# Down products by output block and attention on four PSUM banks in an attention + two-FFN kernel

## The chip, the cores and the metric

The kernel runs on one core of a Trainium2 chip. The metric is the device time of one execution in microseconds (us); lower is better. A profile is one further execution, recorded instruction by instruction. Engines are named as in the profile: PE (TensorE matmul), PEld (its weight loads), DVE (VectorE), ACT (ScalarE), POOL (GpSimd) and SP (the queue that issues nearly all DMAs).

## The reference

Attention over 4 batches of 8 heads (576 positions, 64 wide), whose output, 2304 tokens of 512 features, goes through two gated feed-forward networks in a row; the first normalises its input by RMS. Everything is float32.

```python
def _attn_ref(q, k, v):
    scores = scale * np.matmul(q, k.transpose(0, 1, 3, 2))
    mask_local = (rel >= 0) & (rel < 32)
    mask_strided = (rel >= 0) & (pos[None, :] % 32 == pos[:, None] % 32)
    masks = np.stack([mask_local if h < H // 2 else mask_strided for h in range(H)], axis=0)
    scores = np.where(masks[None], scores, -1000000000.0)
    attn = softmax(scores)
    return np.matmul(attn, v)

def _moe_ref(x, w_gate, w_val, w_out, rms_g):
    xn = x / rms * rms_g
    g = xn @ w_gate
    silu = g * (1.0 / (1.0 + np.exp(-g)))
    return silu * (xn @ w_val) @ w_out
```

The second network is the same without the normalisation. The hidden width is 1536, that is 12 chunks of 128.

## The kernel before, in words

**Products.** Each float32 product is made of three products of a high and a low part (`hi`, `lo`), so a 128x128 block of weights against n tokens is three matmuls. A *chunk* is 128 hidden features: its *gate* products (bank `g`, or `a0` late) and *value* products (bank `v`, or `a1`) are 12 matmuls each, and its *down* products are 3 matmuls for each of the four output blocks j (128 output features, banks `y0` to `y3`).

**Stages.** (1) Attention of batch 0 alone. (2) Attention of batches 1 to 3 woven into chunks 0 to 3 of the first network, which run over six token *segments* (`early`, L39: 256, 256, 512, 512, 256, 512 tokens). (3) What is left: passes over chunks 4 to 11 of the first network and 0 to 11 of the second, in steps of 768 tokens. The first of them (called pass 0 below) follows the last segment at once. Only stage 2 and its border with pass 0 are touched.

**What sets the order in stage 2.** `gate` (L976) and `down` (L998) call `point()` (L176) after every few matmuls. A point is a *place*: there one phase of each running attention step is issued (`advance`, L97), new steps are started as `pace["att"]` allows (0.9 a place in segments 0 and 1, 1.3 from segment 2 on, L1186), one small operation of the x sums in `due` may be issued, and one operation of a weight step of `late` (paced by `pace["op"]`). Every engine then executes its own instructions in the order in which they stand.

**Attention steps.** Scores (S, `kT,qT`), softmax on DVE (L664), ACT (L673), DVE (L683, L684) and POOL (L690), transposes of the softmax `e` (T, L69), their copy to `pT` on ACT (L76), products with v (V, `pT,vl` or `pT,vs`) and their copy to `x`. The transposes of q and k are copied to `qT` and `kT` by ACT and DVE. Each S, T or V takes a bank from `att.tags` in turn (`abank`, L498). In stage 1 these are all eight banks, in stage 2 the two banks `a0` and `a1` (L1080).

**Down products.** `run` (L1090) issues the down products of a chunk two chunks later, all four j on banks `y0` to `y3`, which collect over the four chunks of a segment. After the fourth, `finish` (L1014) copies the four banks to `ob` buffers (DVE for even j, ACT for odd j) and sends them to DRAM; until attention is over, `ob` shares three buffers (tag `s`) with the gate's own temporary `sg`.

**Weights.** `room[4]` is the list of 4 KB places for split weights, 13 at first, 5 more when attention's memory is freed and 2 more before pass 0. `plan` (L1069) lists the weight steps: `d` splits a down weight, `p` splits the seven combined gate and value weights of a chunk and parks them in DRAM (`pk`), `r` recalls them. `ahead_x` (L1112) makes sums of x early, from a pool `px` with two buffers for each of four tags.

Of the kernel before, what the change touches and what calls it, by code (L numbers as in the profile page):

```python
# [8 lines left out]
F32 = mybir.dt.float32  # L9
F32R = mybir.dt.float32r  # L10
# [15 lines left out]
def attn_ffn_ffn(ctx: ExitStack, tc: tile.TileContext, q, k, v, w1g, w1v, w1o, rms_g, w2g, w2v, w2o, out):  # L26
# [38 lines left out]
    def product(out_, a, b_, start, stop, **how):  # L65
        traced(nc.tensor.matmul(out_, a, b_, start=start, stop=stop, **how))  # L66
# [4 lines left out]
    def bank(tag):  # L71
        return pp.tile([128, 512], F32, tag=tag, name=f"b_{tag}")
# [103 lines left out]
    def point():  # L176
        advance()
        if state["early"]:
            some_x()
        weights()  # L180
        for nm, src in (("dec", wq), ("att", steps)):
            if state["hold"] and nm == "dec":
                continue
            have[nm] = min(have[nm] + pace[nm], 2.0)
            while have[nm] >= 1.0 and src and src[0].ready():
                have[nm] -= 1.0
                start(src.pop(0))
# [12 lines left out]
    wt = {}  # L200
    wdone = set()

    room = {4: [(wpa, f"u{i}") for i in range(13)], 2: []}
    held = {}
    order = [(m, c) for m in (1, 2) for c in range(FC)]

# [257 lines left out]
    def need_w(m, c, z):  # L464
        drain(wq, lambda: (m, c, z) in wdone or not wq and not any(st.prio == PRIO_W for st in active))
        while (m, c, z) not in wdone:
            if begun:
                operate(begun[0])
            else:
                prefetch(True)  # L470
# [505 lines left out]
    def gate(m, c, n, xs, final=False):  # L976
        need_w(m, c, 0)
        gv = GV[0]
        GV.append(GV.pop(0))
        pg = bank(gv[0])  # L980
        proj(pg, n, wt[m, c, 0], xs)
        hp, w = pools["h"]
        s = hp.tile([128, w], F32, tag="s", name="sg", bufs=3)
        silu(s, pg, n)
        point()
        need_w(m, c, 1)
        pv = bank(gv[1])
        proj(pv, n, wt[m, c, 1], xs)
        if final:
            hh, hl = (pools["ob"][0].tile([128, 512], F32R, tag="ob", name=nm) for nm in ("hh", "hl"))  # L990
        else:
            hh = hp.tile([128, w], F32R, tag="hh", name="hh", bufs=3)
            hl = hp.tile([128, w], F32R, tag="hl", name="hl", bufs=3)
        hidden(s, pv, hh, hl, n)
        point()
        return hh, hl
# [59 lines left out]
    def plan(text):  # L1056
        for word in text.split():
            m, c = int(word[1]), int(word[2:])
            kind = word[0]
            if kind in "dq":  # L1060
                late.append(weight_step(m, c, 2, kind == "q"))
            elif kind == "s":
                late.append(recall_out(m, c))
            elif kind == "r":
                late.append(recall_step(m, c))
            else:
                late.append(combined_step(m, c, {"c": "keep", "h": "split", "p": "park"}[kind]))

    plan("d14 p14 p15 p16 p17 r14 d15 r15 d16 r16 d17 r17 c18 d18 p19 p110 p111 r19 d19 r110 d110 r111 d111 "  # L1069
         "c20 d20 p21 p22 p23 r21 d21 r22 d22 r23 d23 c24 d24 p25 p26 p27 r25 d25 r26 d26 r27 d27 c28 d28 p29 p210 p211 r29 d29 r210 d210 r211 d211")  # L1070
    att.consts()
    for b in range(B):
# [2 lines left out]
    for i in range(1000):  # L1075
# [1 line left out]
            break  # L1077
        pace["dec"] = 0.7 if i >= 0 else 0.0
        point()
    att.tags = ["a0", "a1"]  # L1080
    state["start"] = False
    waiting = []
    with tc.high_priority(offset=PRIO_R):
# [6 lines left out]
    def run(f):  # L1090
        si, c, h = f
        m, t0, n, c0, c1 = segs[si]
        if c == c0:
            ys[:] = [bank(f"y{j}") for j in range(KC)]
        down(m, c, n, ys, h, c == c0, c == c1 - 1)
        if si == last_seg[m, c]:
            used((m, c, True))
        if c == c1 - 1:
            finish(t0, n, ys)

    def there(si):
        if si >= NA or att is None:
            return True
        t0, n = segs[si][1:3]
        return all((b, j) in att.done for b in range(B) for j in range(2) if S * b + parts(b)[j][0] < t0 + n)
# [6 lines left out]
    def ahead_x(t0):  # L1112

        pool = pools["px"][0]
        f = {}
        xsum[1, t0] = {}

        def fetch_(nm, kk):
            def g():
                t = f[nm, kk] = pool.tile([128, HN], F32, tag=nm, name="xst", bufs=2)  # L1120
                k0, o0 = RAW[nm]
                for o, a, w, d in pieces(x_d, t0 + o0, HN):
                    send(out=t[:, o:o + w], in_=d[:, k0 + kk, a:a + w])
            return 0, g

        def add(z, a, b, op, kk):
            def g():
                paced(nc.gpsimd.tensor_tensor(out=f[z, kk], in0=f[a, kk], in1=f[b, kk], op=op))
            return 1, g

        def keep_(i, nm, kk):
            def g():
                d = xsum[1, t0].setdefault(i, [])
                d.append(dp.tile([128, HN], F32, name=f"xq{t0}_{i}_{kk}"))
                send(out=d[kk], in_=f[nm, kk])
            return 0, g

        rest = 1, lambda: None
        todo = [fetch_(nm, kk) for kk in range(2) for nm in ("a21", "a22", "a11", "a12")] + [rest] * 4
        for kk in range(2):  # L1140
            todo += [add("a22", "a21", "a22", ALU.add, kk), keep_(5, "a22", kk), add("a21", "a11", "a21", ALU.subtract, kk), keep_(7, "a21", kk),
                     add("a11", "a22", "a11", ALU.subtract, kk), keep_(6, "a11", kk), add("a12", "a12", "a11", ALU.subtract, kk), keep_(3, "a12", kk)]
        due.extend((0, cost, g) for cost, g in todo)

    def first_x():
# [37 lines left out]
    for si, (m, t0, n, c0, c1) in enumerate(segs):  # L1183
        nxt = segs[si + 1] if si + 1 < len(segs) else None
        loaded = False
        pace["att"] = 0.9 if si < 2 else 1.3  # L1186
        pace["dec"] = 0.25
        pace["op"] = 0.0 if si < 2 else 1.8
        state["late"] = si >= 2
        state["xr"] = 0.8 if si < NA - 1 else 0.4  # L1190
        state["lag"], state["wait"] = (5, 6) if att is None else (2, 3)
        xs = xs_of.pop(si)
        state["tanh"] = True and att is not None
        for c in range(c0, c1):
            for i, t in enumerate((0, 2 * HN)):
                if att is not None and si >= 2 and (1, t) not in xsum and have_x(t + 2 * HN) and (not i or (1, 0) in xsum):
                    ahead_x(t)
                    state["early"] = True
            if nxt_last(si) and c == 0:
                first_x()  # L1200
                state["early"] = True
            h = gate(m, c, n, xs, nxt is None and c == c1 - 1)
            if si == last_seg[m, c]:
                used((m, c, False))
            if len(waiting) >= 2:
                run(waiting.pop(0))
            waiting.append((si, c, h))
            if att and not steps and not active_att():
                if due: print("due left", len(due))
                while due:  # L1210
                    due.pop(0)[2]()
                actx.close()
                close_pools("px")
                att = None
                GV.append(("a0", "a1"))
                open_pool("wpb", "wpb", 0, bufs=1)
                open_pool("ob", "ob", 512, bufs=4)
                room[4] += [(pools["wpb"][0], f"v{i}") for i in range(5)]
                open_pool("x7", "x7", 0, bufs=1)
                room[2] += [(pools["wpb"][0], f"e{i}") for i in range(5)]  # L1220
            if nxt and c >= c1 - 3 and si + 1 not in xs_of:
                if c == c1 - 2 and not there(si + 1):
                    while steps and not there(si + 1):
                        advance()
                        if steps[0].ready() and not there(si + 1):
                            start(steps.pop(0))
                    while not there(si + 1):
                        advance()
                if not loaded and there(si + 1):
                    load_x(*nxt[:3])  # L1230
                    loaded = c
                if loaded is not False and (c > loaded or c == c1 - 1):
                    xs_of[si + 1] = split_x(si + 1)
# [8 lines left out]
    open_pool("xs", "xs", 0, bufs=1, reuse_waits="tile")  # L1242
    open_pool("ob2", "ob2", 512, bufs=3)
    open_pool("wpc", "wpc", 0, bufs=1)
    room[4] += [(pools["wpc"][0], f"w{i}") for i in range(2)]
    x7, xs, tp, obp, obq = (pools[key][0] for key in ("x7", "xs", "t", "ob", "ob2"))
    SETS = (("g", "v", "a0", "a1"), ("y0", "y1", "y2", "y3"))
    passes = [(1, (4, 5, 6, 7)), (1, (8, 9, 10, 11)), (2, (0, 1, 2, 3)), (2, (4, 5, 6, 7)), (2, (8, 9, 10, 11))]
# [387 lines left out]
```

## Time and profile before

| what | value |
|---|---|
| median of 3 runs | 1060.49 us (1058.42 to 1064.2) |
| the profiled execution's own time | 1058.07 us |
| its span, first to last instruction | 1056.3 us |
| PE busy | 986.0 us (93%) |
| PEld busy | 903.9 us (86%) |
| DVE, ACT busy | 582.8 us, 581.8 us (55% each) |
| POOL busy | 394.8 us (37%) |
| mean granted clock of TensorE | 0.970 of full |

The granted clock has two levels here, 2.4 GHz (written 1.00) and 1.2 GHz; a value between them is a stretch that had both. The time lies 1.8 us above the span, and the profiled execution is 2.4 us below the median. A busy PE is read from the row of the slices; where PE waited, and for whom, is read from the waits; a bracket in the timeline, `[2.38 <-ACT pT L76]`, is the idle time before that instruction and what ended it.

### The profile page before, as it was taken

Reading aid. Unit: us, or ns where it says so; the run is one execution under the profiler, and the core shown is the slowest. Engines: PE = TensorE matmul, PEld = TensorE weight load, DVE = VectorE, ACT = ScalarE, POOL = GpSimd, SP = SyncE. Lnnn points to the kernel's source line nnn. Section 1 sums busy time; section 2 is a strip of 40 time slices with the busy share of each in tenths; the row PEclk is TensorE's granted clock in tenths of the full one; section 3 lists DMA queues with packets and bytes.
Section 4 is the critical chain, followed back from the end, with each engine's and each line's share of the span. In section 5 each row is a group of like instructions: output and inputs, shape, how many; then the busy total and the mean of one; then the engine's idle time right before and its main releaser. Section 6 shows DMA issues by size and latency. Waiting matters only on the chain. (4 is left out here: it accounts for less than half of the span.)

```text
span 1056.3 us, 17050 instructions
## 1 busy us (share of the span) xinstructions
PE 986.0 (93%) x5768; PEld 903.9 (86%) x5768; DVE 582.8 (55%) x1297; ACT 581.8 (55%) x1457; POOL 394.8 (37%) x421
## 2 busy tenths in 40 slices
PE   4759988897999999999999999999999999999998
PEld 4548976676798999998999999999998999988997
DVE  3766476565653464546564566654556655563433
ACT  5876675566535464546555456655556555563431
POOL 3212135162105152815253473846335252522400
PEclk9759999989999999999999999999999999999999
DMA  7566265582498647599575959538687567875121
GB/s 193 157 191 193 64 182 190 171 264 85 164 326 285 230 139 251 171 330 308 159 248 171 324 200 320 177 127 297 221 292 225 196 228 278 301 224 180 62 79 60
DMA packets 169967, 218.19 MB, mean 207 GB/s; under 512 B 46996, under 2 KB 123484, under 8 KB 169880
## 3 DMA queue, kind: packets, MB, share of 16 engines
q1 hardware_dynamic: 169688, 216.83, 62.8%
q8 instruction: 45, 0.74, 0.3%
q14 instruction: 42, 0.34, 0.1%
q0 software_dynamic: 192, 0.28, 0.1%
HBM read 145.23 MB, written 71.83 MB: 205 GB/s over the span
## 5 line engine op out<-in xcount | busy, mean ns | idle before, releaser
L1309 POOL TENSOR_TENSOR xl<-xst,xh 128x384 fp32r<-128x384 f32 x196 | 211.4, 1103 | 190.0 <-ACT xh L1308 85.6
L66 PE MATMUL b_y<-xh,w 128*128 128x384 f32 x784 | 211.7, 336 | 4.2 <-DVE t L1376 1.9
L66 PEld LDWEIGHTS b_y<-xh,w 128*128 128x128 f32 x784 | 142.9, 188 | 8.1 <-DVE t L1376 2.3
L66 PE MATMUL b_a<-xh,w 128*128 128x384 f32 (+2 forms) x512 | 141.9, 336 | 2.2 <-ACT t L1366 0.9
L66 PE MATMUL b_y<-xl,w 128*128 128x384 f32 x392 | 131.4, 335 | 0.0
L66 PE MATMUL b_g<-xh,w 128*128 128x384 f32 (+2 forms) x416 | 127.7, 348 | 1.9 <-ACT t L1366 1.2
L66 PE MATMUL b_v<-xh,w 128*128 128x384 f32 (+2 forms) x352 | 110.2, 354 | 0.0
L66 PE MATMUL b_y<-hh,w 128*128 128x384 f32 (+2 forms) x384 | 104.7, 345 | 0.5 <-ACT hh L1390 0.3
L66 PEld LDWEIGHTS b_a<-xh,w 128*128 128x128 f32 x512 | 93.1, 188 | 6.5 <-ACT t L1366 1.8
L1308 ACT CAST xh<-xst 128x384 fp32r<-128x384 f32 x196 | 91.6, 520 | 2.5 <-DMA xst<-x_d 2.5
L66 PE MATMUL b_a<-xl,w 128*128 128x384 f32 (+2 forms) x256 | 85.9, 335 | 0.0
L66 PEld LDWEIGHTS b_g<-xh,w 128*128 128x128 f32 x416 | 77.0, 190 | 7.1 <-ACT t L1366 1.7
L374 POOL TENSOR_TENSOR raw<-dh 128x256 f32<-128x256 f32 x40 | 29.0, 740 | 142.5 <-DVE dh L285 86.5
L66 PEld LDWEIGHTS b_y<-xl,w 128*128 128x128 f32 x392 | 73.6, 188 | 1.7
L66 PEld LDWEIGHTS b_y<-hh,w 128*128 128x128 f32 x384 | 70.0, 191 | 5.9 <-ACT hh L1390 0.6
L690 POOL TENSOR_TENSOR e<-e,rc 128x384 f32<-128x384 f32 (+3 forms) x40 | 38.1, 954 | 94.2 <-DVE rc L684 40.4
L66 PE MATMUL b_g<-xl,w 128*128 128x384 f32 (+2 forms) x208 | 70.5, 339 | 0.0
L66 PEld LDWEIGHTS b_v<-xh,w 128*128 128x128 f32 x352 | 65.5, 191 | 5.2 <-issue 0.4
L66 PE MATMUL b_y<-w,hh 128*128 128x512 f32 x216 | 67.6, 393 | 0.5 <-DVE w L297 0.5
L280 DVE SCALAR_TENSOR_TENSOR raw<-raw 128x512 uint32<-128x512 uint32 x53 | 48.1, 911 | 34.5 <-ACT raw L276 34.4
L66 PE MATMUL b_y<-hl,w 128*128 128x384 f32 (+2 forms) x192 | 65.4, 341 | 0.0
L673 ACT ACTIVATE e<-e,nb 128x96 f32<-128x96 f32 (+2 forms) x152 | 56.4, 375 | 13.9 <-DVE nb L664 13.8
(206 smaller groups left out, 2114.2 us busy)
## 6 DMA issues: line engine op xcount, KB each, us to landing
w<-pk SPq DMA_DIRECT2D x48, 512.0 KB
pk<-raw SPq DMA_DIRECT2D x80, 256.0 KB
raw<-in_moe_w_gate_dram SPq DMA_DIRECT2D x24, 512.0 KB
raw<-in_moe_w_val_dram SPq DMA_DIRECT2D x24, 512.0 KB
raw<-in_moe_w_out_dram SPq DMA_DIRECT2D x24, 512.0 KB
part<-ob SPq DMA_DIRECT2D x48, 256.0 KB
xst<-y_d SPq DMA_DIRECT2D x30, 384.0 KB
xst<-xq SPq DMA_DIRECT2D x28, 384.0 KB
```

What stands on the lines that cost most here:

```text
L66: traced(nc.tensor.matmul(out_, a, b_, start=start, stop=stop, **how))
L280: nc.vector.scalar_tensor_tensor(out=cell["r"], in0=cell["hw"], scalar=0x80000000, in1=cell["r"], op0=ALU.bitwise_and, op1=ALU.bitwise_or)
L374: paced(nc.gpsimd.tensor_tensor(out=t[:, z], in0=a, in1=b, op=ALU.subtract))
L673: r = nc.scalar.activation(out=e[:qn, i, :kn], in_=e[:qn, i, :kn], func=AF.Exp, bias=nb[:qn, i:i + 1], scale=-1.0, accum_out=sums[:qn, i:i ...
L690: eng.tensor_tensor(out=e[:qn, :nt, :kn], in0=e[:qn, :nt, :kn], in1=rc[:qn, :nt].unsqueeze(2).to_broadcast([qn, nt, kn]), op=ALU.mult)
L1308: nc.scalar.copy(out=xh[:, kk], in_=src[:, kk])
L1309: nc.gpsimd.tensor_tensor(out=xl[:, kk], in0=src[:, kk], in1=xh[:, kk].bitcast(F32), op=ALU.subtract)
```

## The change

1. `att.tags` in stage 2 becomes `a0, a1, y2, y3`: four banks for attention.
2. Down products are collected per segment (`kept`) and issued by `by_block` behind the next segment's first gated chunk: for each output block j the 12 matmuls of all four chunks, on `y0` for even j and `y1` for odd j, then that block's copy and store. The last segment keeps the old way. `hh` and `hl` get five buffers instead of three.
3. `pace["att"]` is 1.1 in segments 0 and 1 and 1.7 from segment 2 on.
4. To pay for the buffers, `px` has one buffer per tag (its two halves one after the other, with rests between), and `room[4]` has 12 places at first, 4 more after attention and 4 more before pass 0. Since the thirteenth place is gone, `d14` stands behind `r14` in the plan.

```diff
-    room = {4: [(wpa, f"u{i}") for i in range(13)], 2: []}
+    room = {4: [(wpa, f"u{i}") for i in range(12)], 2: []}
-            hh = hp.tile([128, w], F32R, tag="hh", name="hh", bufs=3)
-            hl = hp.tile([128, w], F32R, tag="hl", name="hl", bufs=3)
+            hh = hp.tile([128, w], F32R, tag="hh", name="hh", bufs=5)
+            hl = hp.tile([128, w], F32R, tag="hl", name="hl", bufs=5)
-    plan("d14 p14 p15 p16 p17 r14 d15 r15 d16 r16 d17 r17 c18 d18 p19 p110 p111 r19 d19 r110 d110 r111 d111 "
+    plan("p14 p15 p16 p17 r14 d14 d15 r15 d16 r16 d17 r17 c18 d18 p19 p110 p111 r19 d19 r110 d110 r111 d111 "
-    att.tags = ["a0", "a1"]
+    att.tags = ["a0", "a1", "y2", "y3"]
+    def by_block(si, hs_):
+        m, t0, n, c0, c1 = segs[si]
+        for j in range(KC):
+            y = bank(f"y{j % 2}")
+            sl = slice(128 * j, 128 * j + 128)
+            for c, (hh, hl) in zip(range(c0, c1), hs_):
+                need_w(m, c, 2)
+                ot = wt[m, c, 2]
+                fh, fl = ot[:, 0], ot[:, 1]
+                for z, (a, b_) in enumerate(((fh[:, sl], hh[:, :n]), (fh[:, sl], hl[:, :n]), (fl[:, sl], hh[:, :n]))):
+                    product(y[:, :n], a, b_, start=c == c0 and z == 0, stop=c == c1 - 1 and z == 2)
+                if c in (c0 + 1, c1 - 1):
+                    point()
+            finish(t0, n, {j: y}, (j,))
...
-                t = f[nm, kk] = pool.tile([128, HN], F32, tag=nm, name="xst", bufs=2)
+                t = f[nm, kk] = pool.tile([128, HN], F32, tag=nm, name="xst")
-        todo = [fetch_(nm, kk) for kk in range(2) for nm in ("a21", "a22", "a11", "a12")] + [rest] * 4
+        todo = []
         for kk in range(2):
+            todo += [fetch_(nm, kk) for nm in ("a21", "a22", "a11", "a12")] + [rest] * 4
...
+            todo += [rest] * 3
-        pace["att"] = 0.9 if si < 2 else 1.3
+        pace["att"] = 1.1 if si < 2 else 1.7
-            if len(waiting) >= 2:
-                run(waiting.pop(0))
-            waiting.append((si, c, h))
+            if c == c0 and kept:
+                by_block(si - 1, kept)
+                kept.clear()
+            if nxt is None:
+                if len(waiting) >= 2:
+                    run(waiting.pop(0))
+                waiting.append((si, c, h))
+            else:
+                kept.append(h)
-                room[4] += [(pools["wpb"][0], f"v{i}") for i in range(5)]
+                room[4] += [(pools["wpb"][0], f"v{i}") for i in range(4)]
-    room[4] += [(pools["wpc"][0], f"w{i}") for i in range(2)]
+    room[4] += [(pools["wpc"][0], f"w{i}") for i in range(4)]
```

How the order moves, at three places. First PE at the start of segment 2, before: the end of the first gate (`b_g`) and the attention steps behind it (`ident,e` is a T, `kT,qT` an S, `pT,vs` a V).

```order
L66 MATMUL b_g_1849<-xh_1845,w1_0_0_212 128x512
L69 MATMUL b_a0_1940<-ident_94,e_1797 126x126 x4
L66 MATMUL b_a1_1945<-kT21_1711,qT21_1686 108x108 x4
L69 MATMUL b_a0_1961<-ident_94,e_1822 126x126 x4
L66 MATMUL b_v_1966<-xh_1833,w1_0_1_246 128x512
...
L66 MATMUL b_a1_1992<-pT_1953,vs2_1395 64x126 x4
L69 MATMUL b_a0_1997<-ident_94,qn20_1770 128x128 x4
```

And in the changed kernel, from the last value products (`b_v`) of segment 1 into the first gate of segment 2:

```order
L69 MATMUL b_a0_1869<-ident_94,e_1757 126x126 x4
L66 MATMUL b_a1_1874<-kT21_1659,qT21_1646 108x108 x4
L66 MATMUL b_g_1879<-xh_1735,w1_0_0_212 128x512
...
L69 MATMUL b_y2_1907<-ident_94,e_1783 126x126 x4
...
L66 MATMUL b_y3_1929<-pT_1883,vs2_1363 64x126 x4
L69 MATMUL b_a0_1934<-ident_94,qn20_1718 128x128 x4
```

Bank `a0` now comes up again after three other banks instead of after one, and the same T, S and V stand about a gate earlier against the segment's own products.

Second, PE at the first down products of segment 0, before: chunk 0 alone, on four banks, three matmuls each.

```order
L66 MATMUL b_y0_1169<-hh_962,w1_0_2_278 128x256
L66 MATMUL b_y0_1169<-hl_963,w1_0_2_278 128x256
...
L66 MATMUL b_y1_1170<-hh_962,w1_0_2_278 128x256
...
L66 MATMUL b_y2_1171<-hh_962,w1_0_2_278 128x256
...
L66 MATMUL b_y3_1172<-hh_962,w1_0_2_278 128x256
```

In the changed kernel, behind segment 1's first chunk: all four chunks on one bank, then the next block.

```order
L66 MATMUL b_y0_1445<-hh_977,w1_0_2_278 128x256
...
L66 MATMUL b_y0_1445<-hh_1080,w1_1_2_426 128x256
...
L66 MATMUL b_y0_1445<-hh_1181,w1_2_2_561 128x256
...
L66 MATMUL b_y0_1445<-hh_1310,w1_3_2_705 128x256
...
L66 MATMUL b_y1_1477<-hh_977,w1_0_2_278 128x256
...
L66 MATMUL b_y0_1507<-hh_977,w1_0_2_278 128x256
```

The third block (`b_y0_1507`) takes the bank of the first, with one block of 12 matmuls between them.

Third, SP around the last segment, before: the recalls (`w1_5`, `w1_6`: chunks 5 and 6) among the loads of x (`xst`) and the stores of the down products (`part1`).

```order
L148 DMA w1_5_0_3826<-pk1_5_0_2607 128x1024
...
L148 DMA w1_5_1_3828<-pk1_5_1_2661 128x1024
L148 DMA xst_3789<-xq0_7_0_2013 128x384
L148 DMA w1_5_2_3830<-pk1_5_2_2771 128x1024
...
L148 DMA w1_6_0_3991<-pk1_6_0_3084 128x1024
L148 DMA part1_1536_1_3914<-ob_3912 128x256
```

And in the changed kernel:

```order
L148 DMA w1_5_0_3924<-pk1_5_0_2522 128x1024
L148 DMA xst_3765<-xq0_7_1_2387 128x384
...
L148 DMA raw_4114<-in_moe_w_gate_dram 128x4x256
L148 DMA part1_1536_3_3870<-ob_3868 128x256
L148 DMA w1_5_1_3926<-pk1_5_1_2560 128x1024
L148 DMA w1_5_2_3928<-pk1_5_2_2701 128x1024
L148 DMA w1_6_0_4038<-pk1_6_0_3042 128x1024
```

The recalls of chunk 5 stand behind the last segment-4 store and a raw load of chunk 8 (`raw_4114`), where before they stood ahead of them.

## Rows read from the trace of the kernel before

**Rows 1.** The page: busy time by engine, and PE in 40 slices of the span.
```profile
PE 986.0 (93%) x5768; PEld 903.9 (86%) x5768; DVE 582.8 (55%) x1297; ACT 581.8 (55%) x1457; POOL 394.8 (37%) x421
...
PE   4759988897999999999999999999999999999998
```

**Rows 2.** By stretch: us, busy PE, PEld, DVE, ACT, POOL, PEclk, DMA share, GB/s.
```profile
77.00:291.00 214.00, 189.39 (x1393) 155.96 (x1390) 127.95 (x466) 133.14 (x442) 68.67 (x78) 0.94 0.54 165
...
291.00:348.00 57.00, 57.00 (x320) 50.09 (x319) 24.70 (x44) 25.07 (x50) 14.62 (x14) 1.00 0.91 310
```

**Rows 3.** PE's waits in 77 to 300 us: us in total, times, longest.
```profile
PE b_a L69 <- ACT pT L76: 5.7, 3, 2.8
PE b_a L69 <- ACT kT L76: 4.7, 2, 4.1
PE b_a L69 <- DVE qT L78: 4.7, 4, 3.1
PE b_a L66 <- ACT pT L76: 2.6, 1, 2.6
PE b_a L66 <- DVE nb L664: 1.6, 2, 1.4
```

**Rows 4.** PE's timeline: start, us, instruction, idle before it and what ended it.
```profile
155.69 0.62 PE L69 MATMUL b_a<-ident,e 126*126 126x126 f32 x4 [2.38 <-ACT pT L76]
170.35 0.97 PE L69 MATMUL b_a<-ident,e 108*108 108x108 f32 x4 [4.07 <-ACT kT L76]
194.29 1.06 PE L69 MATMUL b_a<-ident,e 128*96 128x128 f32 x4 [2.76 <-ACT pT L76]
221.72 1.77 PE L66 MATMUL b_a<-kT,qT 64*108 64x108 f32 x8 [1.39 <-DVE nb L664]
241.45 0.76 PE L69 MATMUL b_a<-ident,qn 128*128 128x128 f32 x4 [3.08 <-DVE qT L78]
263.55 0.69 PE L66 MATMUL b_a<-kT,qT 128*128 128x96 f32 x4 [2.61 <-ACT pT L76]
```

**Rows 5.** ACT's timeline ahead of three of these waits.
```profile
170.03 0.27 ACT L76 COPY kT<-b_a 128x128 f32<-128x128 f32 x1 [4.51 <-DVE qT L78]
...
193.29 0.37 ACT L76 COPY ob<-b_y 128x256 f32<-128x256 f32 x1 [3.30 <-DMA part<-ob]
...
262.40 0.62 ACT L413 CAST raw<-raw 128x512 fp32r<-128x512 f32 x1
262.92 0.58 ACT L76 COPY pT<-b_a 96x512 f32<-96x512 f32 x1
```

**Rows 6.** PE's timeline: down products of 256 and of 512 tokens.
```profile
126.94 0.40 PE L66 MATMUL b_y<-hh,w 128*128 128x256 f32 x2
127.17 0.28 PE L66 MATMUL b_y<-hl,w 128*128 128x256 f32 x1
...
204.59 0.61 PE L66 MATMUL b_y<-hh,w 128*128 128x512 f32 x2
205.05 0.39 PE L66 MATMUL b_y<-hl,w 128*128 128x512 f32 x1
```

**Rows 7.** Copies of down products, 77 to 345 us: count, ns min/median/max, first and last.
```profile
L78 DVE COPY ob<-b_y x10: 418/424/692, 127.3 to 329.1; 128x256 f32<-128x256 f32 x6, 128x512 f32<-128x512 f32 x4
L76 ACT COPY ob<-b_y x10: 360/372/591, 127.7 to 330.7; 128x256 f32<-128x256 f32 x6, 128x512 f32<-128x512 f32 x4
```

**Rows 8.** An issue of a recall of chunk 5, and PE's first product of it.
```profile
321.08 0.38 SPq L148 DMA_DIRECT2D w<-pk  x1
...
356.29 0.33 PE L66 MATMUL b_a<-xh,w 128*128 128x384 f32 x1
```

**Rows 9.** Columns of rows 2, for 10 us around three of the waits.
```profile
150.00:160.00 10.00, 7.62 (x42) 5.63 (x41) 8.37 (x26) 8.43 (x32) 8.66 (x8) 0.83 0.25 69
...
220.00:230.00 10.00, 8.61 (x29) 6.66 (x30) 8.24 (x38) 6.18 (x29) 7.58 (x8) 0.57 0.90 285
...
260.00:270.00 10.00, 7.39 (x74) 5.64 (x73) 5.38 (x17) 7.89 (x27) 1.60 (x2) 1.00 0.60 208
```

More of the change, by code (lines that the diff above doesn't have):

```diff
@@ L1099, in run @@
             finish(t0, n, ys)
+    def by_block(si, hs_):
[12 more added lines that the diff above has]
+            finish(t0, n, {j: y}, (j,))
+        for c in range(c0, c1):
+            if si == last_seg[m, c]:
+                used((m, c, True))
+    kept = []
     def there(si):
```

## The prediction

> **What bounds the kernel now.** I read the page first: PE is busy for 93% of the span, and of its 40 slices only the first dozen, up to some 300 us, fall short of nines [rows 1]. Behind them PE is full and is the bound, so the change can give something only in stages 1 and 2; stage 1 keeps its eight banks and its order, and I leave it at no change. Then the stretches [rows 2]: while attention is woven in (77 to 291 us) PE is busy for 189.4 of 214 us, 24.6 us idle, at a mean granted clock of 0.94. The clock knows two levels, so 0.06 x 214 = 12.8 us are what the stretches at 1.2 GHz cost. The 57 us behind it, up to pass 0, are full at clock 1.00. So 24.6 + 12.8 = 37.4 us is all there is to win.
>
> Third, PE's waits there [rows 3]: the five costliest kinds make 5.7 + 4.7 + 4.7 + 2.6 + 1.6 = 19.3 us. All stand at an attention step that takes bank `a0` or `a1` while the copy of that bank's last content (`pT`, `kT`, `qT`), or the softmax's reading of it (`nb`), is not done. The rest of the idle time is 24.6 - 19.3 = 5.3 us in small pieces. Fourth, PE's timeline [rows 4]: six waits of 1.39 to 4.07 us are most of it. Fifth, what ACT did ahead of three of them [rows 5]: at 170 us it had stood 4.51 us behind a DVE copy of `qT`; at 193 us it had stood 3.30 us before an `ob` copy, because `ob` has three buffers and an earlier store had not landed; at 262 us the `pT` copy that PE wanted stood behind weight casts.
>
> **The change part by part.**
>
> *Four banks.* A bank comes up again after three other steps, not one. Between the two T on `a0` at 155.69 us there was one S; now two or three steps and six to nine of the segment's matmuls at 0.23 us [rows 6] stand between, some 3 us. A wait for the bank alone goes. What stays is where the data itself is late, since the V behind a T needs the `pT` copy in any case. At 170.35 us ACT's whole queue was late by 4.51 us; the V comes 2 to 3 us after its T, so I keep 2.4 of the 4.07 us. At 155.69 us I keep 0.9, at 241.45 us 1.0 and at 263.55 us 0.7 us by the same reasoning, at the others none: 5 of the 19.3 us stay. The bounds are 0 and 19.3.
>
> *Down products by block.* The products are the same, and so are the places: two for each block, eight a segment. A block is 12 matmuls, at 0.12 us 1.4 us with 256 tokens and at 0.23 us 2.8 us with 512 [rows 6], and its bank is needed again one block later. The copy takes 0.37 or 0.42 us [rows 7]. The block between covers that unless the copying engine is over a microsecond late, so I take 0; the bound above is the second rival. The four `ob` copies are no longer made at once, so ACT's 3.30 us [rows 5] and with them PE's 2.76 us at 194.29 us [rows 4] go; they are among the bank waits above.
>
> *More steps per place.* 1.7 for 1.3 from segment 2 on is 1.31 times as much attention per place. ACT is busy for 133 of 214 us, 62% [rows 2]; times 1.31 that is 81% where attention is dense, and the casts of `p15`, `p16` and `p17` come in runs on top. The nearest row for what that does is the wait of 2.61 us behind such casts [rows 4, 5]. I take one wait of about 2.4 us for each of the three chunks, 7 us of new idle time. The bounds are 0 (four banks swallow it) and 19.3 us (each bank wait comes back as a wait for data); I stay nearer the lower end, since ACT is still not full on the mean.
>
> *What moves behind attention.* Attention's last products now stand in segment 3's third chunk, before in its fourth; the gates passed over follow at full clock. That moves PE's work and adds none: 0.
>
> *One `px` buffer per tag.* The second half's fetches wait on SP until the first half's stores have landed, and later loads and stores queue behind them. PE's large waits name no DMA [rows 3], and POOL, which uses these tiles, is busy for 69 of 214 us [rows 2]. I take 0; above, 3.3 us, the nearest row of a wait for a store [rows 5].
>
> *Places for weights, `d14` later.* Recalls of chunks 5 to 7 wait for places that come free about a chunk later. SP issued a part of chunk 5's at 321 us and PE first used that chunk at 356 us [rows 8]: 35 us of lead against 24 x 0.23 = 5.5 us of delay. I take 0, covered by that lead. `d14`'s casts leave the attention stretch; that is within the 7 us.
>
> *Clock.* The 10 us around a wait stand below 1.00 for five of the six (0.83 at 150 us, 0.57 at 220 us), and at 1.00 for the one at 263.55 us [rows 9]. With three new waits of 2.4 us and one kept, I let two of the five low stretches stay, 5 of the 12.8 us, so 7.8 us come back. Bounds: 0 and 12.8 us.
>
> **The sum.** Idle after: 5 + 7 + 5.3 = 17.3 us, 7.3 less. With the clock's 7.8 us that is 15.1 us. The profiled execution took 1058.1 us: 1043.0. It lies 2.4 us below the median of the runs, so for a median I say 1045 us.
>
> **The rivals.**
>
> *The waits move from the banks into ACT's queue.* Rows 5 speak for it: in each of the three cases ACT was late, not only a bank taken. Then only the `ob` burst goes, 2.8 us of idle time and one of five low stretches, 12.8 / 5 = 2.6 us: 1060.5 - 5.4 = 1055 us, from 1051 to 1061 by what becomes of the other waits. Against it: ACT is idle for 38% of the stretch, and a V stands well behind its T. The Trainium skill (PSUM — Partial Sum Buffer, Engine vs sequencer instructions) says that the queues of ScalarE, VectorE and GpSimdE are strictly first in, first out, so more banks let no copy pass the casts ahead of it. By that rule alone the time would be this rival's, 1055 us; the trace agrees on the order at 262 us [rows 5].
>
> *Two banks are too few for the down products, and it gets slower.* The third and fourth block of a segment wait for the copies of the first and second, and these for an engine that is busy with attention, or for a store. It decides once a copy ends later than a block lasts, 1.4 to 2.8 us. At 193 us ACT was 3.30 us late with such a copy [rows 5]. Five segments are done in this way; two waits of 3.3 us in each are 33 us, against 15.1 won: 1060.5 + 18 = 1078 us, and with half of them 1062. Against it: the copies no longer come at once. The Trainium skill (TensorE: Matmul & The Clock Gate, A second HAM failure mode: psum-queue depth-cycling) tells of a kernel that cycled through banks, paused between groups of matmuls and had its clock lowered and raised again and again. By that rule all blocks of these five segments, 48 x (3 x 0.12 + 2 x 0.23) = 39 us of matmuls, could take twice as long; rows 6 show such products at full speed before.
>
> *Pass 0 waits for a recall.* The DMA engines' share is 0.91 in the 57 us before pass 0 [rows 2]. If the chunk's delay shows in full for one of chunks 5 to 7, 5.5 us come back, with some more for a second: about 1052 us.
>
> That the change doesn't do what it says has no chance: the order shows the four banks and the blocks.
>
> **How the numbers follow.** Forecast 0.60, between 1031 (30 of the 37.4 us) and 1053; ACT's queue 0.21, at 1051 to 1061; recalls 0.10, at 1049 to 1056; too few down banks 0.09, at 1062 and above. A measurement of this kernel can tell 0.5% from no change, 5.3 us, so faster is below 1055.2 us and slower above 1065.8 us. Faster: 0.60, 0.09 of the recalls and 0.06 of ACT's queue, 0.75. The same: the rest of these two, 0.16. Slower: 0.09. The range of 1032 to 1060 leaves out the slow rival, the top of ACT's queue and the lowest end of the forecast.
>
> **What would show it.** In the profile of the changed kernel: PE idle in the attention stretch near 17 us at a mean clock near 0.97; attention's last product some 20 us earlier than 291 us; no wait of ACT for `part<-ob` over 1 us; waits for `pT` at a V, not at a T; PE full from there through pass 0's first four chunks. I am wrong if the first products on `b_y` wait for `ob` copies, if the idle time stays at 24 us under other names, if the low-clock stretches stay although the waits are gone, or if PE waits for `w<-pk` in pass 0.

## The result, and the profile after

The changed kernel takes 1036.45 us, the median of 4 runs (1033.64 to 1037.05), beside 1061.83 us of the kernel before in 4 runs (1058.42 to 1064.2): a ratio of 0.9758, 95% interval 0.9724 to 0.9793, so 25.4 us less. Ratios are formed without the runs in which a core was in its slower state, while medians and ranges take in all runs. The forecast was 1045 us: faster, with the time inside the range, but the 15.1 us of the sum were too small by 10 us. The profiled execution took 1036.4 us over a span of 1034.6 us, 21.7 us less than the span before. That difference is traced here. The other 3.7 us lie between the medians and the profiled executions: before stood 2.4 us below the median of its runs when I forecast (3.8 us below the one here), after stands at its own median.

From the page of the changed kernel: the engines' busy time, PE's slices and its granted clock, to be held against [rows 1].

```profile
span 1034.6 us, 17058 instructions
PE 978.8 (95%) x5768; PEld 901.0 (87%) x5768; DVE 585.0 (57%) x1297; ACT 580.2 (56%) x1457; POOL 395.9 (38%) x421
PE   4759989999999999989999999999999999999998
PEclk9759999999999999999999999999999999999999
```

The slices are nines from the fourth on, with few exceptions; before, that took a dozen. The stretches of the changed kernel, to be held against [rows 2] (PE, PEld, DVE, ACT and POOL busy, granted clock, share of the DMA engines, GB/s):

```profile
77.00:270.00 193.00, 184.17 (x1412) 153.84 (x1412) 132.52 (x480) 135.04 (x447) 68.73 (x78) 0.97 0.64 198
270.00:330.00 60.00, 59.35 (x321) 51.93 (x322) 20.06 (x32) 22.81 (x48) 15.30 (x14) 1.00 0.80 271
```

PE is idle for 193 - 184.17 = 8.8 us while attention is woven in, and for 0.65 us in the 60 us behind it: 9.5 us, where it was 24.6. The clock costs 0.03 x 193 = 5.8 us, where it was 12.8. That is 15.1 and 7.0 us less, 22.1 us together; the span fell by 21.7, so 0.4 us were given back elsewhere. The page says nearly the same of the whole span: PE's busy time, for the same 5768 products, fell by 7.2 us, from 986.0 to 978.8, and its idle time by 14.5, from 1056.3 - 986.0 = 70.3 to 55.8 us. Attention's last product begins at 255.1 us, before at 290.2 us (the first line here is of the kernel before):

```profile
290.24 0.68 PE L66 MATMUL b_a<-dg,ones 128*128 128x128 f32 x4 [1.24 <-DVE dg L850]
```

```profile
255.10 0.61 PE L66 MATMUL b_y<-dg,ones 128*128 128x128 f32 x4
```

PE's waits from 77 to 300 us (us in total, times, longest), the list that answers to [rows 3]; three more are of 0.2 us each (`hl`, `kT`, `mean`):

```profile
PE b_a L69 <- POOL e L690: 3.5, 2, 2.3
PE b_g L66 <- DVE xl L961: 1.9, 1, 1.9
PE b_y L69 <- DVE qT L78: 1.3, 1, 1.3
PE b_y L66 <- ACT hh L947: 0.8, 1, 0.8
PE b_v L66 <- DVE sg L944: 0.7, 1, 0.7
PE b_y L66 <- ACT ob L76: 0.7, 1, 0.7
```

Of the waits for a bank, 19.3 us of `pT`, `kT`, `qT` and `nb`, 1.5 us are left. New at the top are two waits for data: a transpose that comes before POOL has scaled its softmax `e`, and a gate of segment 2 that comes before the low part `xl` of its x. The four longest on PE's timeline are of 1.22 to 2.33 us, where [rows 4] had six of 1.39 to 4.07 us:

```profile
140.47 0.65 PE L69 MATMUL b_a<-ident,e 126*126 126x126 f32 x4 [1.22 <-POOL e L690]
146.19 0.78 PE L66 MATMUL b_g<-xl,w 128*128 128x512 f32 x1 [1.88 <-DVE xl L961]
156.21 0.75 PE L69 MATMUL b_y<-ident,e 108*108 108x108 f32 x4 [1.27 <-DVE qT L78]
202.55 0.65 PE L69 MATMUL b_a<-ident,e 126*126 126x126 f32 x4 [2.33 <-POOL e L690]
```

The clock in stretches of 10 us, answering to [rows 9]: from 80 us on only the stretches with these waits are below 1.00, and 220 to 230 us, which was at 0.57, is full at 1.00.

```profile
140.00:150.00 10.00, 7.65 (x40) 5.58 (x41) 5.78 (x17) 6.55 (x26) 6.07 (x6) 0.83 0.22 74
150.00:160.00 10.00, 8.50 (x49) 6.16 (x48) 7.16 (x18) 7.38 (x22) 4.49 (x5) 0.83 0.27 89
200.00:210.00 10.00, 7.67 (x41) 5.85 (x41) 6.18 (x30) 6.62 (x25) 6.72 (x6) 0.83 0.99 289
220.00:230.00 10.00, 10.00 (x84) 8.05 (x83) 6.61 (x32) 10.00 (x43) 6.09 (x8) 1.00 0.45 152
```

### The profile page after: what moved, and what is told of

The parts are those of the page before. It is cut to its first block, busy times and chain, and to the rows that moved or that the text cites. A ratio compares the mean times of both kernels' runs of the same rounds, so it can differ in the third digit from the quotient of the medians.

```text
span 1034.6 us, 17058 instructions
## 1 busy us (share of the span) xinstructions
PE 978.8 (95%) x5768; PEld 901.0 (87%) x5768; DVE 585.0 (57%) x1297; ACT 580.2 (56%) x1457; POOL 395.9 (38%) x421
## 5 line engine op out<-in xcount | busy, mean ns | idle before, releaser
L673 ACT ACTIVATE e<-e,nb 128x96 f32<-128x96 f32 (+2 forms) x152 | 56.8, 379 | 10.2 <-DVE nb L664 10.1
```

The lines of the kernel that those rows point to most:

```text
L673: r = nc.scalar.activation(out=e[:qn, i, :kn], in_=e[:qn, i, :kn], func=AF.Exp, bias=nb[:qn, i:i + 1], scale=-1.0, accum_out=sums[:qn, i:i ...
```

## The experiments

The open question is where the 10 us came from that the sum did not have, and which part carries the rest: the banks, the pace, or both. Four kernels came first: each of the two taken back alone, and the pace and `d14` put alone into the kernel before. Each ratio is to the kernel before on the same chip, with its 95% interval; a median of a few runs on another chip is compared by its ratio.

**Two banks.** Down products still by block.

```diff
-    att.tags = ["a0", "a1", "y2", "y3"]
+    att.tags = ["a0", "a1"]
```

> The changed kernel with attention back on a0 and a1 alone (y2 and y3 lie unused). If the four banks make the gain: nearly all of it goes, PE idle in the attention stretch back to 20 us or more, 1055 to 1065 us. If the spread of the down products' copies and the moved casts make it: at most a third goes, 1036 to 1044 us.

Measured: 1065.01 us (1060.62 to 1073.15), ratio 1.0039 (1.001 to 1.0067). The whole gain is gone. PE's waits, 77 to 300 us:

```profile
PE b_a L69 <- DVE qT L78: 4.0, 4, 2.0
PE b_a L66 <- DVE nb L664: 3.7, 5, 1.1
PE b_a L66 <- ACT kT L76: 3.1, 1, 3.1
PE b_a L69 <- ACT kT L76: 2.0, 1, 2.0
```

These are the kinds of [rows 3]. With 0.9 us for `pT` they make 13.7 us, where the kernel before had 19.3, and PE is idle for 17.5 of the 214 us from 77 to 291 us, not for the 20 or more that I expected. The mean clock there is 0.92, and much of the loss is that: over the whole span PE is busy for 993.2 us with the products that took 978.8 in the changed kernel, and idle for 65.5 us instead of 55.8.

**The old pace.**

```diff
-        pace["att"] = 1.1 if si < 2 else 1.7
+        pace["att"] = 0.9 if si < 2 else 1.3
```

> The changed kernel with 0.9 and 1.3 steps per place. If the banks make the gain and the pace little: 1034 to 1042 us. If the denser attention makes it: 1050 us or more.

Measured: 1063.04 us (1055.92 to 1072.39), ratio 1.0014 (0.9978 to 1.005). The whole gain is gone here too, but by other waits:

```profile
PE b_g L66 <- ACT xh L960: 8.5, 2, 4.7
PE b_y L66 <- DVE ss L820: 7.1, 1, 7.1
PE b_a L66 <- DVE dg L850: 3.7, 4, 3.0
```

No wait for a bank is among the first three. Two gates of 512 tokens wait for the high part `xh` of their x, one at each of two segment borders, and the sums of squares of the RMS (`ss`, and `dg`, which is made from them) come late in between:

```profile
139.49 0.79 PE L66 MATMUL b_g<-xh,w 128*128 128x512 f32 x1 [3.76 <-ACT xh L960]
202.26 1.44 PE L66 MATMUL b_y<-ones,ss 128*128 128x1 f32 x6 [7.14 <-DVE ss L820]
227.63 0.80 PE L66 MATMUL b_g<-xh,w 128*128 128x512 f32 x1 [4.69 <-ACT xh L960]
```

A second effect of `by_block` stands behind this, which I had not seen: with a segment's down products moved behind the next segment's first gate, that gate is issued four places earlier, while the attention that makes its x moves on only with the places passed. The run with two banks and the old pace, below, bears this out.

**The new pace in the kernel before.**

```diff
-        pace["att"] = 0.9 if si < 2 else 1.3
+        pace["att"] = 1.1 if si < 2 else 1.7
```

> The kernel before with 1.1 and 1.7 steps per place alone, on two banks. Banks theory: steps come closer on the same two banks, so no gain or a loss, 1058 to 1070 us. Pace theory: 1045 us or less.

Measured: 1060.1 us (1047.93 to 1066.35), ratio 0.9963 (0.9919 to 1.0007): no difference that can be told. The profiled execution is the slowest of the ten. Waits for the two banks stay (`nb` 7.7 us, `kT` 5.3, `pT` 3.4 and 2.5).

**`d14` behind `r14` in the kernel before.**

```diff
-    plan("d14 p14 p15 p16 p17 r14 d15 r15 ...
+    plan("p14 p15 p16 p17 r14 d14 d15 r15 ...
```

> The kernel before with d14 behind r14 in the plan, so that its casts leave the attention stretch, and nothing else. If such casts in ACT's and DVE's queues were the cause of the waits: 5 us or more faster, 1055 us or less. Banks theory: 0 to 4 us faster, 1057 to 1062 us.

Measured: 1054.58 us (1047.74 to 1065.1), ratio 0.9904 (0.9874 to 0.9934). This small step, which the sum did not price, gives some 1% by itself where attention has two banks: the time that I expected if casts in ACT's and DVE's queues were a cause of the waits. Its profile does not say how: the span is 1057.4 us, against 1056.3 before, with waits for `qT` of 6.2 us and for `pT` of 4.8 and 1.7.

The next four fill the square of banks and pace and change sizes.

**Two banks and the old pace in the changed kernel.**

```diff
-    att.tags = ["a0", "a1", "y2", "y3"]
+    att.tags = ["a0", "a1"]
...
-        pace["att"] = 1.1 if si < 2 else 1.7
+        pace["att"] = 0.9 if si < 2 else 1.3
```

> The changed kernel with both put back: two banks and 0.9 and 1.3 steps per place; the down products by block, the buffers and the weight places stay. If banks and pace only help together, because the later down products leave fewer places ahead of a segment's end: 1060 to 1070 us, PE waiting for the next segment's x. If one of the two alone had been harmful: below 1056 us.

Measured: 1068.06 us (1064.35 to 1077.96), ratio 1.0088 (1.0057 to 1.0119). Of the two cases expected it is the first. `d14` has moved in this kernel too, so the rest of the layout (down products by block, their buffers, `px`, the places) costs 1.0088 - 0.9904 = 1.8% of the time while banks and pace are as before. Among PE's waits from 77 to 300 us are two kinds for a segment's x that the kernel before does not have at all, and that the kernel with two banks and the new pace does not have either:

```profile
PE b_g L66 <- ACT xh L960: 6.3, 2, 3.7
PE b_g L66 <- DVE xl L961: 2.1, 3, 1.5
```

This fits `by_block`, which issues these gates earlier; that the loads for `px` have a part in it was not tried. The faster pace alone removes these waits. The square for the changed layout, as ratios:

| | old pace | new pace |
|---|---|---|
| two banks | 1.0088 | 1.0039 |
| four banks | 1.0014 | 0.9758 |

Four banks alone give 0.7%, the pace alone 0.5%, both 3.3%: of those 3.3, 2.1 are to be had only together. The waits say why: with two banks, steps brought forward meet a taken bank; with four banks at the old pace, the gates wait for x and the steps for `ss` and `dg`. That four banks alone would help the kernel before can't be tried, as its down products take all four `y` banks.

**Three banks.**

```diff
-    att.tags = ["a0", "a1", "y2", "y3"]
+    att.tags = ["a0", "a1", "y2"]
```

> The changed kernel with attention on a0, a1 and y2. If each bank adds reach: between the two, 1042 to 1056 us. If three steps of distance already cover the copies: 1034 to 1040 us.

Measured: 1045.89 us (1042.69 to 1049.47), ratio 0.9874 (0.9819 to 0.9929): about half the gain. Waits for a bank are down already, `kT` 1.3 us and `qT` 0.9; the longest wait of the profiled execution is one for data, 6.37 of 7.5 us:

```profile
211.12 1.10 PE L69 MATMUL b_a<-ident,e 126*126 126x126 f32 x4 [6.37 <-POOL e L690]
```

Yet that wait is not where its time went: over the span PE is idle for 57.4 us, 1.6 more than in the changed kernel, and busy for 6.0 more. More on this is said at the end of the section.

**One bank for the down products, five for attention.**

```diff
-    att.tags = ["a0", "a1", "y2", "y3"]
+    att.tags = ["a0", "a1", "y1", "y2", "y3"]
...
-            y = bank(f"y{j % 2}")
+            y = bank("y0")
```

> The changed kernel with all blocks of the down products on y0, and y1 given to attention as a fifth bank. Each block after the first then waits for the copy of the one before, at least 0.4 us for 15 blocks, and 1 us and more where ACT or DVE is behind: 1042 to 1060 us if a block of cover is what makes two banks enough; 1034 to 1038 us if the copies are in time anyway or the fifth bank pays for them.

Measured: 1054.55 us (1049.54 to 1070.23), ratio 0.9943 (0.9903 to 0.9983). Three quarters of the gain are gone, and here are the copies that I had priced at nothing:

```profile
PE b_y L66 <- DVE ob L78: 8.0, 7, 2.9
PE b_a L69 <- POOL e L690: 5.8, 2, 4.6
PE b_y L66 <- ACT ob L76: 2.7, 4, 1.6
```

Eleven waits, 10.7 us, for `ob`; with two banks it is one of 0.7 us. The block between is the cover that the prediction named, and this is what it costs if that is gone.

**Faster still.**

```diff
-        pace["att"] = 1.1 if si < 2 else 1.7
+        pace["att"] = 1.4 if si < 2 else 2.2
```

> The changed kernel with 1.4 and 2.2 steps per place. If the time left comes from steps too thin: 1030 to 1035 us. If ACT and DVE are now the limit where attention is dense, waits for data grow: 1037 to 1050 us.

Measured: 1054.44 us (1047.53 to 1061.36), ratio 0.9954 (0.9924 to 0.9984), slower than either case expected. Now steps stand on PE ahead of their data:

```profile
PE b_a L69 <- ACT x L76: 4.1, 1, 4.1
PE b_a L66 <- DVE dg L850: 3.8, 2, 3.5
PE b_a L69 <- POOL e L690: 3.0, 1, 3.0
```

So the best pace lies between the old one and this. The last four kernels take the pace apart.

**The old pace in segments 0 and 1 alone.**

```diff
-        pace["att"] = 1.1 if si < 2 else 1.7
+        pace["att"] = 0.9 if si < 2 else 1.7
```

> The changed kernel with the old pace of 0.9 in segments 0 and 1 alone (1.7 from segment 2 on stays). Theory: with four banks the faster pace pays because the next segment's x must be ready four places earlier than before; both segment borders lose at the old pace (8.5 us behind xh in two waits, 7.1 us behind ss). With the early half alone undone, segment 2's first gate (about 139 us) waits for xh again, 3 to 4 us, and low-clock stretches follow; segment 3's border is made up by the 1.7: about 1048 us. Rival (only the total progress of attention counts, so the late half carries all of it): no such wait, within 5 us of the changed kernel, 1036 to 1041 us. Second rival (the early half carries all): 1060 us or more.

Measured: 1060.35 us (1056.94 to 1066.81), ratio 1.0011 (0.9984 to 1.0038). The second rival comes true: with the early half undone the whole gain is gone, and 1.7 makes up nothing. PE's waits from 77 to 300 us:

```profile
PE b_g L66 <- ACT xh L960: 8.1, 2, 4.6
PE b_a L66 <- DVE dg L850: 7.9, 1, 7.9
PE b_g L66 <- DVE xl L961: 3.8, 1, 3.8
```

The wait of 7.9 us can be followed through two more engines. PE's, DVE's and ACT's timelines around it:

```profile
203.38 1.18 PE L66 MATMUL b_a<-dg,ones 128*128 128x128 f32 x3 [7.87 <-DVE dg L850]
```

```profile
193.37 0.16 DVE L842 TENSOR_SCALAR mean<-b_y 128x3 f32<-128x3 f32 x1
201.56 0.69 DVE L280 SCALAR_TENSOR_TENSOR raw<-raw 128x512 uint32<-128x512 uint32 x1 [8.02 <-ACT raw L276]
...
202.95 1.66 DVE L850 TENSOR_SCALAR dg<-ident,rstd 128x128 f32<-128x128 f32 x3
```

```profile
200.86 0.67 ACT L276 ACTIVATE raw<-raw 128x512 uint32<-128x512 uint32 x1 [8.14 <-DMA raw<-in_moe_w_val_dram]
```

ACT stands for 8.14 us at a weight step whose load has not landed, DVE stands at the next operation of that step, and `dg`, whose `mean` was there at 193.5 us, stands behind it in DVE's queue. SP issued that load only at 195.99 us. In the changed kernel SP issued it at 182.61 us, and ACT's operation on it (L276, the fourth of its kind from 100 us on in both kernels) at 186.15 us does not wait. The products of `dg` run at 186.0 us, and do not wait either:

```profile
186.03 0.89 PE L66 MATMUL b_a<-dg,ones 128*128 128x128 f32 x6
```

```profile
186.15 0.73 ACT L276 ACTIVATE raw<-raw 128x512 uint32<-128x512 uint32 x1
```

Why SP comes to that load 13 us later at the old pace was not followed further.

**The old pace from segment 2 on alone.**

```diff
-        pace["att"] = 1.1 if si < 2 else 1.7
+        pace["att"] = 1.1 if si < 2 else 1.3
```

> The changed kernel with the old pace of 1.3 from segment 2 on alone (1.1 in segments 0 and 1 stays). Theory: segment 2's start is fed as in the changed kernel, segment 3's first gate (about 227 us) waits for xh again, some 4 to 5 us, and a softmax or dg wait of some 3 us may stand in segment 2: about 1050 us. Rival (late half is of no use once the early half is there): 1036 to 1041 us. Second rival (late half carries all): 1060 us or more.

Measured: 1043.75 us (1040.74 to 1050.05), ratio 0.9865 (0.9834 to 0.9897). Half the gain stays: faster than the 1050 us that I expected, slower than the rival's 1041. The profiled execution is the slowest of the five, and in it no gate waits for `xh`, against what I expected; the waits are for `e` (4.0 and 3.6 us), one `x` (2.3 us) and `xl` (1.9 us). With the run before: the early half is worth 2.5% where the late half is there (1.0011 against 0.9758) and 1.5% where it is not (1.0014 against 0.9865); the late half 1.1% or nothing.

**1.5 instead of 1.7.**

```diff
-        pace["att"] = 1.1 if si < 2 else 1.7
+        pace["att"] = 1.1 if si < 2 else 1.5
```

> The changed kernel with 1.5 instead of 1.7 from segment 2 on. If 1.7 is more than four banks need, as the wait of 2.3 us for the softmax's e at 202 us suggests, the wait goes and the time is 1032 to 1036 us. If segment 3's start is the limit, a wait for xh of 1 to 3 us appears at about 225 us: 1038 to 1045 us.

Measured: 1042.72 us (1034.63 to 1050.23; without the slowest of the five up to 1044.34), ratio 0.9815 (0.9773 to 0.9858). The time is that of the second case, but not by its wait: no wait for `xh` appears, and the wait for `e` keeps its 2.33 us, at 204.58 us. The profile has three waits for `e`, 5.3 us, where the changed kernel has two, of 3.5 us.

**1.2 instead of 1.1.**

```diff
-        pace["att"] = 1.1 if si < 2 else 1.7
+        pace["att"] = 1.2 if si < 2 else 1.7
```

> The changed kernel with 1.2 instead of 1.1 in segments 0 and 1. If segment 2's start still wants its x earlier (wait of 1.9 us for xl at 146 us), that wait goes and the time is 1032 to 1036 us. If a faster pace brings steps out before their data, as 1.4 and 2.2 did (1054 us), waits for x, dg or e of 3 to 6 us appear: 1040 to 1048 us.

Measured: 1045.28 us (1038.05 to 1047.58), ratio 0.9866 (0.9834 to 0.9898). The wait for `xl` is gone, as the first case has it, but the time is the second's. Two waits for `e` (6.2 us) and one for `qT` (2.8 us) are longer than in the changed kernel, but they are not the reason: over the span PE is idle for 54.7 us, there for 55.8. The span's 8.9 us more are the clock. In the first 23 us of stage 2, with PE full, it stood at 0.56, in the changed kernel at 1.00; 0.44 x 23 = 10.1 us:

```profile
77.00:100.00 23.00, 23.00 (x117) 20.61 (x117) 10.28 (x60) 11.79 (x49) 6.71 (x6) 0.56 0.60 170
```

No kernel that I tried is shown to be faster than the changed one. 1.5 can't be told from it for certain, as the two intervals overlap.

**What these profiles can't tell.** The clock of those 23 us differs from one profiled execution to the next: 1.00 in the kernel before, the changed one and the old early pace, 0.65 with two banks, 0.69 with three, 0.70 with the old late pace. In the last of these it cannot come from the edit, which acts only from segment 2 on; whether it comes from the edit in the others, no run shows. It is worth up to 10 us. So the medians and intervals above carry the comparisons of banks and pace, and the waits carry the mechanism where PE's idle time differs clearly: 70.2 us at the old pace and 71.5 at the old early pace, against 55.8. For three banks, the old late pace and 1.2, that the waits make the whole difference is not shown.

## Why the prediction was right, and where its size was off

*Four banks*: right in kind. 19.3 us of waits for a bank became 1.5, where I had kept 5; with the banks taken back they are 13.7. The 2.4 us that I kept at 170.35 us, because the V would find its `pT` late, did not come: no V waits for `pT`.

*More steps per place*: the 7 us of new waits for data came as 5.4, `e` and `xl`, but not as I had reasoned from ACT's share of 62%: they end with POOL and DVE, none with a copy or cast on ACT. The longest, for `e` at 202.55 us, stands behind DVE. ACT had the exponentials of this `e` done at 196.7 us; DVE, busy without a gap from 194.3 us, came to their reciprocals at 201.11 us, and POOL scaled `e` from there:

```profile
201.11 0.18 DVE L684 RECIPROCAL rc<-sums 126x4 f32<-126x4 f32 x1
```

```profile
201.46 3.75 POOL L690 TENSOR_TENSOR e<-e,rc 126x504 f32<-126x504 f32 x4 [6.86 <-DVE sums L683]
```

What the term had wrong is the pace taken as a cost alone. Taking it back makes the kernel slower by 26.6 us (1063.04 less 1036.45; 2.6% by the ratios), and the waits that come back are for x and `ss`: `by_block` issues each next segment's gate earlier, and at the old pace its x is not ready by then; steps that come late also ended up behind a weight operation that held ACT for 8.14 us. The forecast put down nothing for that loss, and so nothing for what the pace gives back.

*The sum*: I had 5 + 7 + 5.3 = 17.3 us of idle time; it is 9.5, made of 1.5 for banks, 5.4 for `e` and `xl`, and 2.6 in small pieces. The small pieces, which I left at 5.3, halved as well; no run says which part of the change did that. The clock, 7.8 us forecast, gave 7.0: three low stretches stayed, not two.

*Down products by block*: 0 was right, one wait of 0.7 us. The copies of segment 2's blocks are no longer made at once but some 2 to 4 us apart (the last two begin at 239.00 and 242.81 us), and no `part<-ob` stands among ACT's waits:

```profile
233.90 0.67 DVE L78 COPY ob<-b_y 128x512 f32<-128x512 f32 x1
```

```profile
235.81 0.59 ACT L76 COPY ob<-b_y 128x512 f32<-128x512 f32 x1
```

The rival on this, two banks too few, does not hold with two and holds with one: 10.7 us. The Trainium skill (TensorE: Matmul & The Clock Gate, A second HAM failure mode: psum-queue depth-cycling) tells of a clock lowered again and again where TensorE pauses between such groups of products. No run here shows it for these blocks: those of segments 0 to 2 begin at 112, 162 and 227 us, in stretches of 10 us in which PE is busy for all 10 and the clock is 1.00.

*The rival of ACT's queue*: not on ACT here, though the wait for `e` just shown is of its kind on DVE; on both at the old early pace, as the chain of 8.14, 8.02 and 7.87 us shows. The Trainium skill (PSUM — Partial Sum Buffer, Engine vs sequencer instructions) has these queues strictly first in, first out; the three timelines agree, on DVE as on ACT.

*What moves behind attention*: 0 was right. Attention ends 35 us earlier, where I said some 20, and behind it PE is idle for 2.4 of the 74 us up to 330 us.

*Places for weights*: 0 was nearly right. One wait for a recall is there, but late, between 920 and 940 us and not in pass 0:

```profile
PE b_a L66 <- DMA w<-pk: 1.3, 1, 1.3
```

*`d14`* I had put within the 7 us; alone, in the kernel before, it gives 1%. What it gives in the changed kernel was not tried, as its thirteenth place is gone there, and by which wait it gives it stays open; so some of what is put down to banks and pace here can be its share. `px`'s one buffer and the places were not tried alone either; no wait names them but the 1.3 us.

So the mechanism of the forecast held in its first half: the waits for banks go, and with them most of the low clock. The 10 us missed are some 3.5 of the banks, 2.7 of the small pieces and 1.6 of the waits for data, less 0.8 of the clock and the 0.4 given back: 6.6 us of span. The other 3.7 us are between the medians and the profiled executions. That the time still lies inside the range is owed to the range's width: 1036.45 us is 8.6 below the forecast and 4.5 above the low end.

## What to carry to other kernels

Where a small stage is woven into a full one, ask of each edit not only how long an engine is busy but which operation it puts ahead of which: a busy share of 62% on ACT did not show the waits that came, which stood behind DVE, behind x and behind a late load. When consumers move forward in the order, their producers must move as well, and the two edits together can give several times what either gives alone, so an experiment that undoes one of them says little about its share. Down products on two banks in turn cost almost nothing here, as one block of 12 matmuls stood between a bank's last product and its next; on one bank they cost 10.7 us of waits.

## What the runs showed of the hardware that I had not expected

The granted clock differs between executions where the products are the same. The kernel with the old late pace has the changed kernel's products on PE in the same order up to 100 us. In the first 23 us of stage 2 PE was full in both profiled executions, and the clock was 1.00 in the changed kernel and 0.70 in the other: 0.30 x 23 = 6.9 us, as much as several of the terms above.

```profile
77.00:100.00 23.00, 22.98 (x194) 20.75 (x195) 17.74 (x92) 18.54 (x77) 8.38 (x9) 1.00 0.76 215
```

```profile
77.00:100.00 23.00, 23.00 (x142) 20.74 (x141) 13.44 (x67) 14.71 (x58) 6.66 (x6) 0.70 0.63 172
```

In stage 1, where PE is idle for some 31 of 77 us, a lower clock cost nothing that can be seen: it was 0.76 in the changed kernel and 0.71 at the old pace, and the first gate begins at 76.06 and 76.22 us.

The runs of one kernel also spread: 13.8 us for the pace of 1.4 and 2.2 in 10 runs, 9.9 us for the old early pace in 11, 3.4 us for the changed kernel in only 4. A single profile need not show what the median shows.
